# First MLP, combined pairs of weight tiles: four PSUM banks, another order of products, one tile of 1024 columns for the four results

## The chip, the cores and the metric

One core of one Trainium2 chip runs the whole program. The metric is the device time of one execution in microseconds (us); below 0.2% (about 3.4 us) two times of this kernel cannot be told apart.

## The reference

```python
# linear attention with an RMS norm, x is [4608, 512]
kv  = einsum('bhsd,bhse->bhde', k, v);  o = einsum('bhsd,bhde->bhse', q, kv)
x   = o / sqrt(mean(o*o) + 1e-6) * g_norm          # heads side by side
# first MLP, 512 -> 2048 -> 512
h   = x @ w_in
x   = (h * clip(h + 3, 0, 6) / 6) @ w_out
# second MLP, 512 -> 1536 -> 512
out = (silu(x @ w_gate) * (x @ w_val)) @ w_out2
```

## The kernel before

All matrix products that need accuracy are made of three products of a high and a low part (hi and lo) of each operand. The helper `split` makes the two: ScalarE (ACT) writes hi (L109), VectorE (DVE) writes lo as the difference (L110).

The first MLP goes through nine blocks of 512 tokens, j = 0 to 8. Block 0, and the first half of block 1, multiply weight tile by weight tile (`h_whole`, L119). From there on two weight tiles (a pair, p) and the two halves of a block are multiplied together by a scheme of seven products in place of eight (`hpair`), on sums and differences of the operands (A11, S1, ... of the weights, made by `combine`; B11, T1, ... of the block, made by `prepare_x1`). There are 60 such pairs: four in block 1, eight in each of the blocks 2 to 8.

A product (`product`, L654) is six matmuls of 256 columns into one PSUM bank. `hpair` works with three banks a, c and d out of the pool `pmm`, which has four; the fourth is free for the attention of the next block. Seven products run in the order a, c, a, d, c, a, d. ACT copies the first results out of a and c into s, v and u (L566, L568, L570), DVE adds d to v (L572), and at the end four adds on DVE (L576 to L579) form the four quarters of the result in two tiles h0 and h1 of 512 columns. Bank a is used three times: the product S2 x T2 adds onto the first one as soon as s has been copied, and A12 x B21 starts anew as soon as u has been copied.

Each of the two tiles is then gated: ACT computes t = relu(h + 3) (L582), DVE computes min(t, 6) * h (L583), and `split_g` makes hi and lo of it, the operand g of the second matrix product `o_pair` (L113 to L115, 24 matmuls of 512 columns for one pair). There is one buffer of t, and three of g.

The order of TensorE's (PE's) work is written out by hand; that of ACT and DVE comes from a planner at build time, and each engine then runs its list strictly in order. On PE, iteration i of a block issues `hpair` of pair i, then a piece of the attention of the next block (at i = 0, 1, 3 and 4 the matmuls `kv` of a head pair, L253, where the next block opens a new batch, and at i = 1, 2, 4 and 5 `at`, both into banks of `pmm`), then `o_pair` of pair i - 1. At i = 0 there is no `o_pair`, so pair 1 of a block follows pair 0 at once, or with only `kv` between them. At the last i, `o_pair` comes twice, and `prepare_x1` of the next block is issued between the two. `kv` is read out of its bank by two splits of 64 x 64, one for each head (ACT, DVE, ACT, DVE). In the last block, j = 8, each iteration also loads, decodes and combines a part of the second MLP's weights on ACT and DVE (`load_second`), and the first operands of the second MLP are prepared (`prepare_x`, L625).

The second MLP's `quad` does the same seven products with four banks of its own, 384 columns wide, and takes two of `hpair`'s tiles as scratch.

Of the kernel before, what the change touches and what calls it, by code (L numbers as in the profile page):

```python
# [8 lines left out]
F32 = mybir.dt.float32  # L9
F32R = mybir.dt.float32r  # L10
U32 = mybir.dt.uint32
AF = mybir.ActivationFunctionType
ALU = mybir.AluOpType
# [5 lines left out]
def kernel(  # L19
# [27 lines left out]
    nc = tc.nc  # L47
    P = 128
# [9 lines left out]
    TQ = T // 2  # L58
# [7 lines left out]
    TH = 384  # L66
    T2 = 2 * TH
# [29 lines left out]
    hpool = ctx.enter_context(tc.tile_pool(name="h1", bufs=1, side="right"))  # L97
# [3 lines left out]
    pmm = mlp1.enter_context(tc.tile_pool(name="pmm", bufs=4, space=PSUM))  # L101


    def f32(ap):
        return ap.bitcast(F32)

    def split(hi, lo, src):

        nc.scalar.activation(out=hi, in_=src, func=AF.Copy)  # L109
        nc.vector.tensor_tensor(out=lo, in0=src, in1=f32(hi), op=ALU.subtract)  # L110
# [16 lines left out]
    three = const.tile([P, 1], F32, name="three")  # L127
# [285 lines left out]
    def split_g(j, f, src):  # L413
        g = gpool.tile([P, 2, T], F32R, tag="g", name=f"g_{j}_{f}")
        split(g[:, 0], g[:, 1], src)
        g_t[j, f] = g
# [131 lines left out]
    def product(ps, w, x, first):  # L548
        n = 0
        for kk in range(2):  # L550
            for a, b in ((w[0], x[1]), (w[1], x[0]), (w[0], x[0])):
                nc.tensor.matmul(
                    ps, a[:, kk], b[:, kk], start=first and n == 0, stop=n == 5,
                    skip_group_check=True,
                )
                n += 1

    def hpair(j, p):

        n = f"{j}_{p}"  # L560
        h = [hpool.tile([P, 2, TQ], F32, tag=f"h{i}", name=f"h{i}_{n}") for i in range(2)]
        s, u, v = (hpool.tile([P, TQ], F32, tag=o, name=f"{o}_{n}") for o in "suv")
        a, c, d = (pmm.tile([P, 512], F32, tag="mm", name=f"{o}_{n}")[:, :TQ] for o in "acd")
        w, x = ready[p], xo1
        product(a, w["A11"], x["B11"], True)
        nc.scalar.activation(out=s, in_=a, func=AF.Copy)  # L566
        product(c, w["S1"], x["T1"], True)
        nc.scalar.activation(out=v, in_=c, func=AF.Copy)  # L568
        product(a, w["S2"], x["T2"], False)
        nc.scalar.activation(out=u, in_=a, func=AF.Copy)  # L570
        product(d, w["S3"], x["T3"], True)
        nc.vector.tensor_tensor(out=v, in0=v, in1=d, op=ALU.add)  # L572
        product(c, w["S4"], x["B22"], False)
        product(a, w["A12"], x["B21"], True)
        product(d, w["A22"], x["T4"], False)
        nc.vector.tensor_tensor(out=h[0][:, 1], in0=u, in1=c, op=ALU.add)  # L576
        nc.vector.tensor_tensor(out=h[0][:, 0], in0=s, in1=a, op=ALU.add)  # L577
        nc.vector.tensor_tensor(out=h[1][:, 1], in0=v, in1=u, op=ALU.add)
        nc.vector.tensor_tensor(out=h[1][:, 0], in0=u, in1=d, op=ALU.add)  # L579
        for i in range(2):  # L580
            t = hpool.tile([P, 2, TQ], F32, tag="t", name=f"t_{n}")
            nc.scalar.activation(out=t, in_=h[i], func=AF.Relu, bias=three[:, 0:1])  # L582
            nc.vector.scalar_tensor_tensor(  # L583
                out=t, in0=t, scalar=6.0, in1=h[i], op0=ALU.min, op1=ALU.mult
            )
            split_g(j, 2 * p + i, t.rearrange("p n c -> p (n c)"))

    def hpair_whole(j, p):
        h_whole([2 * p], j)
# [70 lines left out]
    def quad(name, w, xo):  # L660

        h = big["h"].tile([P, 4, TH], F32, tag="h", name=f"h{name}")
        u, v = (hpool.tile([P, TH], F32, tag=f"h{i}", name=f"h{i}{name}") for i in range(2))

        a, e, c, d = (
            big["ps"].tile([P, 512], F32, tag=f"q{i}", name=f"q{i}_{name}")[:, :TH] for i in range(4)
        )
        product(c, w["S1"], xo["T1"], True)
        product(d, w["S3"], xo["T3"], True)
        nc.scalar.activation(out=v, in_=c, func=AF.Copy)  # L670
        nc.vector.tensor_tensor(out=v, in0=v, in1=d, op=ALU.add)
        product(a, w["A11"], xo["B11"], True)
        nc.scalar.activation(out=u, in_=a, func=AF.Copy)
        product(e, w["S2"], xo["T2"], True)
        nc.vector.tensor_tensor(out=u, in0=u, in1=e, op=ALU.add)
        product(c, w["S4"], xo["B22"], False)
        product(d, w["A22"], xo["T4"], False)
        nc.vector.tensor_tensor(out=h[:, 3], in0=v, in1=u, op=ALU.add)
        nc.vector.tensor_tensor(out=h[:, 1], in0=u, in1=c, op=ALU.add)
        nc.vector.tensor_tensor(out=h[:, 2], in0=u, in1=d, op=ALU.add)  # L680
        product(a, w["A12"], xo["B21"], False)
        nc.scalar.activation(out=h[:, 0], in_=a, func=AF.Copy)  # L682
        return h

    def gv_step(c, j, p, xo):
        hg = quad(f"g_{c}", wgv["g", p], xo)
        nc.scalar.activation(out=hg, in_=hg, func=AF.Silu)
        hv = quad(f"v_{c}", wgv["v", p], xo)
        nc.vector.tensor_tensor(out=hv, in0=hg, in1=hv, op=ALU.mult)  # L689
        nc.sync.dma_start(  # L690
            out=g2d[2 * p:2 * p + 2, :, j * T2:(j + 1) * T2].rearrange("f p t -> p f t"),
            in_=hv.rearrange("p (f n) c -> p f (n c)", f=2),
        )
# [152 lines left out]
    with tc.manual_schedule(engines={mybir.EngineType.PE}):  # L846
# [13 lines left out]
        for h in range(2):  # L860
            nc.sync.dma_start(
                out=gn[h * D:(h + 1) * D, :], in_=g_norm.rearrange("(p o) -> p o", o=1)
# [145 lines left out]
        for j in range(1, NB):  # L1008
# [3 lines left out]
            for i, p in enumerate(pairs):  # L1012
                if j == 1 and p < PWHOLE:
                    hpair_whole(j, p)
                    make_wi(p + PWHOLE)
                    if p == PWHOLE - 1:
                        prepare_x1(j)
                else:
                    hpair(j, p)
                    if j == 2 and i < PWHOLE:  # L1020
                        make_wi(i)
# [64 lines left out]
        for c, (n, j, p) in enumerate(steps):  # L1086
            i = c % NH
# [8 lines left out]
            if n < NB2:  # L1096
                m = (n + 1) % NB2
                if i < 2:
                    tiles = load_half(*halves[m], i)
                    if i and m:  # L1100
                        for k, t in enumerate(tiles):
                            nc.sync.dma_start(
                                out=wsd[m - 1, k], in_=f32(t).rearrange("p k f -> p (k f)")
# [81 lines left out]
```

## Time and profile before

| | us |
|---|---|
| median of 3 runs | 1703.4 (1702.52 to 1703.5) |
| the profiled execution's own time | 1705.95 |
| its span, first to last instruction | 1704.2 |
| PE busy | 1668.5 (98%) |
| DVE busy | 1321.0 (78%) |
| ACT busy | 813.8 (48%) |
| granted TensorE clock, mean | 0.996 |

An engine's busy time counts its instructions, overlaps once. PEld is the loading of weights into TensorE, which runs beside the matmuls; a matmul that has to wait shows first as a wait of its weight load. The first MLP's combined pairs stand between 198 and 888 us of the span, the last block of them between 796 and 888 us.

### The profile page before, as it was taken

Reading aid. Unit: us, or ns where it says so; the run is one execution under the profiler, and the core shown is the slowest. Engines: PE = TensorE matmul, PEld = TensorE weight load, DVE = VectorE, ACT = ScalarE, POOL = GpSimd, SP = SyncE. Lnnn points to the kernel's source line nnn. Section 1 sums busy time; section 2 is a strip of 40 time slices with the busy share of each in tenths; the row PEclk is TensorE's granted clock in tenths of the full one; section 3 lists DMA queues with packets and bytes.
Section 4 is the critical chain, followed back from the end, with each engine's and each line's share of the span. In section 5 each row is a group of like instructions: output and inputs, shape, how many; then the busy total and the mean of one; then the engine's idle time right before and its main releaser. Section 6 shows DMA issues by size and latency. Waiting matters only on the chain.

```text
span 1704.2 us, 27886 instructions
## 1 busy us (share of the span) xinstructions
PE 1668.5 (98%) x10608; PEld 1522.4 (89%) x10608; DVE 1321.0 (78%) x2531; ACT 813.8 (48%) x1489; POOL 2.4 (0%) x7
## 2 busy tenths in 40 slices
PE   7999999999999999999999999999999999999999
PEld 3566789899988989998889999999999999999998
DVE  5897987777777767776889988778898677877774
ACT  4565554445445454545555544443554444443432
POOL 0000000000000000000000000000000000000000
PEclk8999999999999999999999999999999999999999
DMA  7886444454544544425454544485444457555643
GB/s 191 246 258 189 128 145 129 129 161 114 164 131 144 143 149 113 128 99 173 161 186 167 216 161 161 148 278 204 149 178 156 142 204 277 198 193 192 215 147 103
DMA packets 224951, 288.63 MB, mean 169 GB/s; under 512 B 80944, under 2 KB 139312, under 8 KB 224816
## 3 DMA queue, kind: packets, MB, share of 16 engines
q1 hardware_dynamic: 224816, 286.85, 52.4%
q8 instruction: 83, 1.36, 0.3%
q14 instruction: 52, 0.43, 0.1%
HBM read 211.03 MB, written 75.76 MB: 168 GB/s over the span
## 4 chain that ended last, share of the span: by engine, by line
PE 81%; DVE 10%; DMA 4%; ACT 3%; issue 2%; SPq 1%; DVEq 0%; ACTq 0%
PE q_g L654 15%; PE q_v L654 14%; PE acc L113 7%; PE acc L114 7%; PE acc L115 7%; PE a L654 6%; PE d L654 4%; PE c L654 4%; PE h L119 3%; PE o2d L795 3%; PE o2a L795 3%; PE o2c L795 3%; PE o2e L795 1%; DMA gb<-g2d 1%; PE kv L253 1%
## 5 line engine op out<-in xcount | busy, mean ns | idle before, releaser
L113 PE MATMUL acc<-g,wo 128*128 128x512 f32 x512 | 202.1, 395 | 0.0
L114 PE MATMUL acc<-g,wo 128*128 128x512 f32 x512 | 199.9, 390 | 0.0
L115 PE MATMUL acc<-g,wo 128*128 128x512 f32 x512 | 199.5, 390 | 0.0
L582 ACT ACTIVATE t<-h,three 128x512 f32<-128x512 f32 x120 | 86.7, 723 | 138.9 <-DVE h L577 109.4
L109 ACT ACTIVATE g<-t 128x512 fp32r<-128x512 f32 x144 | 90.9, 631 | 87.4 <-DVE t L583 73.4
L110 DVE TENSOR_TENSOR g<-t,g 128x512 fp32r<-128x512 f32 x144 | 98.0, 681 | 31.5 <-ACT g L109 31.2
L115 PEld LDWEIGHTS acc<-g,wo 128*128 128x128 f32 x512 | 96.1, 188 | 20.5
L113 PEld LDWEIGHTS acc<-g,wo 128*128 128x128 f32 x512 | 96.2, 188 | 20.0
L114 PEld LDWEIGHTS acc<-g,wo 128*128 128x128 f32 x512 | 96.2, 188 | 18.3
L583 DVE SCALAR_TENSOR_TENSOR t<-t,h 128x512 f32<-128x512 f32 x120 | 82.6, 689 | 19.3 <-ACT t L582 15.7
L119 PE MATMUL h<-x,w_i 128*128 128x512 f32 x192 | 87.0, 601 | 1.9 <-DVE w_i L173 1.9
L119 PEld LDWEIGHTS h<-x,w_i 128*128 128x128 f32 x192 | 36.7, 193 | 43.2 <-issue 40.2
L682 ACT ACTIVATE hg<-q_g 128x384 f32<-128x384 f32 x36 | 17.8, 494 | 117.1 <-PE q_g L654 117.1
L654 PE MATMUL q_v<-hT,v 128*128 128x384 f32 x288 | 73.6, 336 | 0.0
L110 DVE TENSOR_TENSOR lT<-T,hT 128x384 fp32r<-128x384 f32 (+1 forms) x120 | 68.0, 588 | 0.8 <-ACT hT L109 0.2
L654 PE MATMUL a<-lB,wh_i 128*128 128x256 f32 x240 | 68.1, 284 | 0.0
L654 PE MATMUL a<-hB,wh_i 128*128 128x256 f32 x240 | 67.9, 283 | 0.0
L654 PE MATMUL a<-hB,wl_i 128*128 128x256 f32 x240 | 67.9, 283 | 0.0
L572 DVE TENSOR_TENSOR v<-v,d 128x256 f32<-128x256 f32 x60 | 25.1, 419 | 54.3 <-PE d L654 54.1
L689 DVE TENSOR_TENSOR hv<-hg,hv 128x1536 f32<-128x1536 f32 x36 | 63.1, 1754 | 5.1 <-ACT hv L682 4.9
L109 ACT ACTIVATE hT<-T 128x384 fp32r<-128x384 f32 (+1 forms) x120 | 60.5, 548 | 2.7 <-DVE T L625 2.5
L682 ACT ACTIVATE hv<-q_v 128x384 f32<-128x384 f32 x36 | 17.8, 494 | 87.2 <-PE q_v L654 87.2
(558 smaller groups left out, 5448.0 us busy)
## 6 DMA issues: line engine op xcount, KB each, us to landing
wo<-wod SPq DMA_DIRECT2D x128, 512.0 KB, 3.5
g2d<-hv SPq DMA_DIRECT2D x36, 768.0 KB, 3.5
graw<-g2d SPq DMA_DIRECT2D x26, 1024.0 KB, 7.3
xr<-x1d SPq DMA_DIRECT2D x11, 1536.0 KB, 7.0
gb<-g2d SPq DMA_DIRECT2D x54, 256.0 KB, 5.4
x1d<-x1o SPq DMA_DIRECT2D x36, 256.0 KB, 3.6
out_dram<-o SPq DMA_DIRECT2D x36, 256.0 KB, 2.5
raw_i<-in_moe_w_in_dram SPq DMA_DIRECT2D x16, 512.0 KB, 5.6
```

Of the source, the lines that this page charges most:

```text
L109: nc.scalar.activation(out=hi, in_=src, func=AF.Copy)
L110: nc.vector.tensor_tensor(out=lo, in0=src, in1=f32(hi), op=ALU.subtract)
L113: nc.tensor.matmul(out_, wh, xl, start=start, stop=False)
L114: nc.tensor.matmul(out_, wl, xh, start=False, stop=False)
L115: nc.tensor.matmul(out_, wh, xh, start=False, stop=stop)
L119: nc.tensor.matmul(out_, f32(w), f32(x), start=start, stop=stop)
L582: nc.scalar.activation(out=t, in_=h[i], func=AF.Relu, bias=three[:, 0:1])
L583: nc.vector.scalar_tensor_tensor(out=t, in0=t, scalar=6.0, in1=h[i], op0=ALU.min, op1=ALU.mult)
L654: nc.tensor.matmul(ps, a[:, kk], b[:, kk], start=first and n == 0, stop=n == 5, skip_group_check=True,)
L682: nc.scalar.activation(out=h[:, 0], in_=a, func=AF.Copy)
L689: nc.vector.tensor_tensor(out=hv, in0=hg, in1=hv, op=ALU.mult)
L795: nc.tensor.matmul(ps[:, i * TO2:(i + 1) * TO2], a[:, cs], b, start=first and i == 0 and n == 0, stop=n == 2, skip_group_check=True,)
```

## The change

`hpair` takes all four banks of `pmm`: S2 x T2 gets a bank e of its own, and A12 x B21 adds onto A11 x B11 in bank a, so that the copy s is gone. The order of the products becomes c, d, a, e, c, d, a. ACT copies v, u and, after the last product, the first quarter; DVE adds d to v, e to u, then v + u, u + c and u + d. The four quarters lie in one tile h of 1024 columns with one buffer, and v is its last quarter. The gate is one operation of 1024 columns on ACT and one on DVE, on one tile t with one buffer. The SBUF that these tiles take is the same in sum (9 KB per partition). `quad`'s scratch tiles take other names, since h0 and h1 no longer exist.

```diff
-        h = [hpool.tile([P, 2, TQ], F32, tag=f"h{i}", name=f"h{i}_{n}") for i in range(2)]
-        s, u, v = (hpool.tile([P, TQ], F32, tag=o, name=f"{o}_{n}") for o in "suv")
-        a, c, d = (pmm.tile([P, 512], F32, tag="mm", name=f"{o}_{n}")[:, :TQ] for o in "acd")
+        h = hpool.tile([P, 4, TQ], F32, tag="h", name=f"h_{n}")
+        u, v = hpool.tile([P, TQ], F32, tag="u", name=f"u_{n}"), h[:, 3]
+        e, c, d, a = (pmm.tile([P, 512], F32, tag="mm", name=f"{o}_{n}")[:, :TQ] for o in "ecda")
         w, x = ready[p], xo1
-        product(a, w["A11"], x["B11"], True)
-        nc.scalar.activation(out=s, in_=a, func=AF.Copy)
         product(c, w["S1"], x["T1"], True)
         nc.scalar.activation(out=v, in_=c, func=AF.Copy)
-        product(a, w["S2"], x["T2"], False)
-        nc.scalar.activation(out=u, in_=a, func=AF.Copy)
         product(d, w["S3"], x["T3"], True)
         nc.vector.tensor_tensor(out=v, in0=v, in1=d, op=ALU.add)
+        product(a, w["A11"], x["B11"], True)
+        nc.scalar.activation(out=u, in_=a, func=AF.Copy)
+        product(e, w["S2"], x["T2"], True)
+        nc.vector.tensor_tensor(out=u, in0=u, in1=e, op=ALU.add)
         product(c, w["S4"], x["B22"], False)
-        product(a, w["A12"], x["B21"], True)
         product(d, w["A22"], x["T4"], False)
-        nc.vector.tensor_tensor(out=h[0][:, 1], in0=u, in1=c, op=ALU.add)
-        nc.vector.tensor_tensor(out=h[0][:, 0], in0=s, in1=a, op=ALU.add)
-        nc.vector.tensor_tensor(out=h[1][:, 1], in0=v, in1=u, op=ALU.add)
-        nc.vector.tensor_tensor(out=h[1][:, 0], in0=u, in1=d, op=ALU.add)
+        nc.vector.tensor_tensor(out=v, in0=v, in1=u, op=ALU.add)
+        nc.vector.tensor_tensor(out=h[:, 1], in0=u, in1=c, op=ALU.add)
+        product(a, w["A12"], x["B21"], False)
+        nc.vector.tensor_tensor(out=h[:, 2], in0=u, in1=d, op=ALU.add)
+        nc.scalar.activation(out=h[:, 0], in_=a, func=AF.Copy)
+        t = hpool.tile([P, 4, TQ], F32, tag="t", name=f"t_{n}")
+        nc.scalar.activation(out=t, in_=h, func=AF.Relu, bias=three[:, 0:1])
+        nc.vector.scalar_tensor_tensor(
+            out=t, in0=t, scalar=6.0, in1=h, op0=ALU.min, op1=ALU.mult
+        )
         for i in range(2):
-            t = hpool.tile([P, 2, TQ], F32, tag="t", name=f"t_{n}")
-            nc.scalar.activation(out=t, in_=h[i], func=AF.Relu, bias=three[:, 0:1])
-            nc.vector.scalar_tensor_tensor(
-                out=t, in0=t, scalar=6.0, in1=h[i], op0=ALU.min, op1=ALU.mult
-            )
-            split_g(j, 2 * p + i, t.rearrange("p n c -> p (n c)"))
+            split_g(j, 2 * p + i, t[:, 2 * i:2 * i + 2].rearrange("p n c -> p (n c)"))
...
-        u, v = (hpool.tile([P, TH], F32, tag=f"h{i}", name=f"h{i}{name}") for i in range(2))
+        u, v = (hpool.tile([P, TH], F32, tag=o, name=f"{o}{name}") for o in ("h", "t"))
```

## Rows read from the trace of the kernel before

**Rows 1.** The page, engines: busy us, share of the span, instructions.
```profile
PE 1668.5 (98%) x10608; PEld 1522.4 (89%) x10608; DVE 1321.0 (78%) x2531; ACT 813.8 (48%) x1489; POOL 2.4 (0%) x7
```

**Rows 2.** Table by stage: length, busy us of each engine (instructions), granted clock, DMA.
```profile
230.00:796.00 566.00, 563.36 (x3807) 508.41 (x3806) 417.81 (x941) 273.27 (x548) 0.00 (x0) 1.00 0.47 136
796.00:888.00 92.00, 85.85 (x531) 76.92 (x530) 75.64 (x158) 50.52 (x96) 0.00 (x0) 1.00 0.51 173
888.00:1704.00 816.00, 806.15 (x5294) 799.96 (x5292) 643.04 (x1044) 364.35 (x609) 0.00 (x0) 1.00 0.53 185
```

**Rows 3.** Waits of weight loads, 190 to 232 us: total us, times, longest.
```profile
PEld a L654 <- ACT s L566: 1.3, 3, 0.6
```

**Rows 4.** Waits of weight loads, 232 to 796 us.
```profile
PEld a L654 <- ACT s L566: 2.5, 5, 0.5
PEld d L654 <- DVE v L572: 2.0, 4, 0.6
```

**Rows 5.** Waits of weight loads, 796 to 890 us (block 8).
```profile
PEld d L654 <- DVE v L572: 4.4, 3, 1.7
PEld a L654 <- ACT s L566: 2.9, 3, 1.7
```

**Rows 6.** PE timeline, block 6 begins at 617.69: start us, us, instruction.
```profile
606.78 0.40 PE L113 MATMUL acc<-g,wo 128*128 128x512 f32 x1
...
617.69 0.28 PE L654 MATMUL a<-lB,wh_i 128*128 128x256 f32 x1
...
619.12 0.30 PE L654 MATMUL a<-lT,wh_i 128*128 128x256 f32 x1
619.26 0.28 PE L654 MATMUL a<-hT,wl_i 128*128 128x256 f32 x1
...
622.82 0.57 PE L253 MATMUL kv<-vA,kA 128*64 128x64 f32 x12
...
623.55 0.39 PE L654 MATMUL a<-lB,wh_i 128*128 128x256 f32 x1
```

**Rows 7.** ACT timeline of the same stretch.
```profile
618.60 0.38 ACT L566 ACTIVATE s<-a 128x256 f32<-128x256 f32 x1 [0.79 <-PE a L654]
...
622.73 0.72 ACT L582 ACTIVATE t<-h,three 128x512 f32<-128x512 f32 x1 [2.29 <-DVE h L577]
623.67 0.22 ACT L109 ACTIVATE kvbd<-kv 64x64 fp32r<-64x64 f32 x1 [0.22 <-PE kv L253]
624.21 0.63 ACT L109 ACTIVATE g<-t 128x512 fp32r<-128x512 f32 x1 [0.32 <-DVE t L583]
624.86 0.22 ACT L109 ACTIVATE kvbd<-kv 64x64 fp32r<-64x64 f32 x1
```

**Rows 8.** DVE timeline of the same stretch.
```profile
624.87 0.69 DVE L110 TENSOR_TENSOR g<-t,g 128x512 fp32r<-128x512 f32 x1 [0.57 <-ACT g L109]
625.60 0.23 DVE L110 TENSOR_TENSOR kvbd<-kv,kvbd 64x64 fp32r<-64x64 f32 x1
```

**Rows 9.** Instructions by line and form: busy us, mean ns, idle before.
```profile
L109 ACT ACTIVATE g<-t 128x512 fp32r<-128x512 f32 x144 | 90.9, 631 | 87.4 <-DVE t L583 73.4 <-DVE t L427 11.9 <-PE acc L115 1.0
L582 ACT ACTIVATE t<-h,three 128x512 f32<-128x512 f32 x120 | 86.7, 723 | 138.9 <-DVE h L577 109.4 <-DVE g L110 29.3
L583 DVE SCALAR_TENSOR_TENSOR t<-t,h 128x512 f32<-128x512 f32 x120 | 82.6, 689 | 19.3 <-ACT t L582 15.7
L110 DVE TENSOR_TENSOR gxl<-gt,gxh 128x1024 fp32r<-128x1024 f32 x26 | 31.8, 1224 | 7.8 <-ACT gxh L109 7.8
L109 ACT ACTIVATE gxh<-gt 128x1024 fp32r<-128x1024 f32 x26 | 27.4, 1054 | 47.5 <-DVE gt L723 47.5
```

**Rows 10.** DVE timeline of block 8.
```profile
801.06 0.56 DVE L625 TENSOR_TENSOR T<-xr 128x384 f32<-128x384 f32 x1 [3.81 <-DMA x1d<-x1o]
801.54 0.41 DVE L572 TENSOR_TENSOR v<-v,d 128x256 f32<-128x256 f32 x1
...
819.68 0.42 DVE L572 TENSOR_TENSOR v<-v,d 128x256 f32<-128x256 f32 x1
```

## Prediction

> **What bounds the kernel now.** The page's first part: PE is busy 98% of the span, DVE 78%, ACT 48% [rows 1]. The table by stage says where the other 2% could be had. Between 230 and 796 us, in the pairs of the blocks 1 to 7, PE stands idle 566.00 - 563.36 = 2.6 us, while DVE has 148 us free and ACT 293; in block 8 (796 to 888) PE is idle 6.2 us of 92, with DVE busy 82%; behind it, in the second MLP, PE is idle 10 us of 816 [rows 2]. The clock is full in all three. So what the change does to the load of ACT and DVE is worth nothing by itself: it has to remove waits of PE, and what it removes there reaches the end, since PE is filled after it.
>
> Next the waits, read at the weight loads, because a late product shows there in full. In the pairs they name two instructions: the second product into bank a waits for the copy s, and A22 x T4 into bank d waits for v + d. From 190 to 232 us s takes 1.3 us (3 times) [rows 3]; from 232 to 796 us s 2.5 us (5 times) and v + d 2.0 us (4 times) [rows 4]; in block 8 v + d 4.4 us (3 times) and s 2.9 us (3 times) [rows 5]. Together 13.1 us: this is all that the pairs could give, 0.8% of the time.
>
> Last the timelines around the start of a block, the **seam**, where pair 1 follows pair 0 without an `o_pair` between them. A product takes (619.12 - 617.69) / 2 = 0.72 us, seven take 5.04, so pair 0 ends at 622.73; `kv` follows and pair 1 starts at 623.55 [rows 6]. Elsewhere an `o_pair` of (617.69 - 606.78) / 2 = 5.45 us stands between two pairs [rows 6]. ACT works at the seam through the gate of pair 0 and the splits of `kv`, and so comes late to the copy s of pair 1. I put the five waits of 0.5 us for s [rows 4] there: one for each of the blocks 2 to 6, the ones whose seam has a `kv`.
>
> **The change part by part.**
>
> *Instructions.* PE keeps its 42 matmuls in each pair. Three copies on ACT stay three, five adds of 256 columns on DVE stay five. The two gate operations on ACT are 2 x 723 = 1446 ns; the one of 1024 columns I estimate as 723 plus what a copy grows by from 512 to 1024 columns, 1054 - 631 = 423: 1146 ns [rows 9]. On DVE 2 x 689 = 1378 become 1224 ns, the row of another two-operand instruction of 1024 columns [rows 9]. Saved are 0.30 and 0.15 us a pair, 18 and 9 us over 60 pairs, on engines that are not the bound: 0. No DMA is added or moved, on no queue. The scratch of `quad` has other names and the same single buffers: 0.
>
> *Bank e and the order, inside a pair.* S2 x T2 no longer waits for any copy. v, u and v + d now have three products (2.16 us) between what they read and the product that needs the bank again; before it was one for s and two for the others. Removed: the waits for s from 190 to 232 us, 1.3; the waits for v + d up to 796 us, 2.0, none of which is longer than 0.6, under the 0.72 of the added product. A third sum: the first matmul of S2 x T2 is followed 0.14 us later by the next, where the spacing is 0.12 [rows 6], the copy s landing just in time; 0.02 to 0.03 us in some 50 pairs, 1.3 us. Together 4.6 us, with 3 and 5 as its ends.
>
> *Block 8, outside its seam.* There v + d is late because DVE has a queue of decoding in front of it (at 819.68 us in pair 2 [rows 10]), not because of its own operand. The order of the products asks for d at the sixth place instead of the seventh, 0.72 us earlier, and one more product follows it. If DVE's list stays as it is, each of these waits grows by 0.72 and the product behind it is moved out: a loss of about 0.35 us a pair. If the planner, which now has v + d ready 1.44 us earlier, puts it before the backlog, the wait goes. One wait of each kind belongs to the block's seam, where v + d runs late at 801.54 us [rows 10]; I give these two about a third of the sums, 1.4 and 0.8, which leaves 5.1 us of waits for the rest of the block [rows 5]; I take 40%, 2.0 us, with -1 and 5.1 as the ends.
>
> *What is late next: the seam.* Here the change adds two waits.
>
> First, v is now a quarter of h, which has one buffer: the copy v of pair 1 may not start before DVE's gate of pair 0 has read h. The chain, on the clock of [rows 6]: the last product ends at 622.73; the copy of the first quarter starts 0.2 us later (as s does: 617.69 + 0.72 = 618.41 to 618.60 [rows 7]) and takes 0.38, to 623.31; the gate's ACT half, after 0.1, to 624.56; DVE's half, after 0.05, to 625.83; v from 625.9 to 626.3. The fifth product of pair 1 needs it at 623.55 + 4 x 0.72 = 626.43. That just holds if nothing stands before v on ACT; but the two splits of g, 0.63 each [rows 7], become ready at the same 625.83, and whatever of them goes first delays v, and behind it u, the first quarter's copy and with them PE: 0 to 1.1 us. In the blocks 7 and 8 there is no `kv`, pair 1 starts 0.8 us earlier, and the wait is 0.7 to 1.9 us.
>
> Second, the banks. Before, pair and `kv` together used the four banks. Now pair 0 uses all, `kv` takes one of them, and pair 1 asks for all four within its first four products, the last of which starts at 625.71. `kv`'s bank is freed in turns of ACT, DVE, ACT, DVE; it came free at 625.60 + 0.23 = 625.83 [rows 8], with DVE's gate of 689 ns in front of it. With 1224 ns in front the first DVE turn falls behind 625.83 and ends at 626.05; the second turns add 0.5 if they go at once, and 1.8 behind a split of g on each engine (0.63 and 0.69 [rows 7, 8]): 626.55 to 627.9. Fourth asker: 0.85 to 2.2 us late; third asker: 0.7 more, up to 2.9. This wait covers the first one. I take 1.4 us, in the lower half because the planner did put `kv`'s splits between those of g [rows 7].
>
> Away from the seam `o_pair`'s 5.45 us cover both chains. At the end of a block `o_pair` of the last pair asks for g 5.45 us after the pair's end; the longer gate (0.2 + 0.38 + 0.1 + 1.15 + 1.22, then 0.63 and 0.69 for hi and lo) gives it at 4.5: free, with 1 us to spare.
>
> *The sum.* Blocks 1 to 7: -4.6. Block 8 outside the seam: -2.0. Five seams with `kv`: 1.4 in place of 0.5, +4.5. Seam of block 7: +1.1, the middle of 0.7 to 1.9 less something. Seam of block 8: +0.5, since 2.2 us of waits stand there already, where DVE stood 3.81 us for a DMA [rows 10]. Sum: -0.5 us. The profiled span of 1704.2 becomes 1703.7 and its own time 1705.95 about 1705.4; that execution was 2.5 us above the median of 1703.4, which becomes **1702.9**. With a seam wait of s us the change is about 6.6 - 1.6 + 2.5 - 5s = 7.5 - 5s us faster.
>
> **A rule against the trace.** The waits of the pairs come back in the same place, at the second use of bank a, 8 times up to 796 us [rows 3, 4]. The Trainium skill, page "Perfetto Trace Analysis", section "Optimizing Tensor Performance", says that independent groups of matmuls should rotate through different PSUM banks so that the evacuation of one overlaps the next group's matmuls. By that, bank e takes away every wait for s and the change gains up to the 13.1 us. It speaks as well against the change: with all four banks in one pair there is nothing left to rotate into for `kv` and the next pair.
>
> **The rivals.**
>
> *The seam is cheap* (faster). The planner puts `kv`'s splits ahead of DVE's gate, or v ahead of g's splits, and s is about 0.4: 5.5 us faster, 1698. For it: ACT and DVE both had idle time of 0.2 to 0.6 us just there [rows 7, 8]. Against it: what the program writes first, the gate, went first before.
>
> *Every wait goes*, as by the rule above: 13.1 + 1.3 us, 1689. For it: each wait names an operation that gets more room. Against it: block 8's queue on DVE [rows 2, 10].
>
> *The seam decides* (slower). `kv`'s bank is the third asked for, and both splits of g go before its last turns: s = 2.9, 7.5 - 14.5 = 7 us slower, 1710. For it: one buffer of h, and a pool with no free bank. It decides from s = 2.2 on (3.4 us slower).
>
> *Block 8 keeps its waits*: -1 in place of 2.0, the sum 3 us worse, 1706, not to be told from no change.
>
> **How the numbers follow.** A measurement of this kernel can tell 0.2%, 3.4 us, from no change. Within it (my forecast with block 8 either way, own range 1700 to 1706.8): 0.38. The cheap seam 0.27 and every wait gone 0.05: faster 0.32. The dear seam: 0.30. The range for 8 in 10 runs from the cheap seam with most of block 8's waits gone (1696) to the dear one (1710).
>
> **What would show it.** After the change no weight load waits for s, and those for v + d up to 796 us are gone. At the seams of the blocks 2 to 6 PE waits in pair 1: for the split of `kv` or for v, and how long is s. In block 8 the count and length of waits for v + d tell whether DVE's list changed. The stage from 888 us to the end stays at 816 us; if it grows, a gain was given back there. Wrong would be the sum, not the size of its terms, if the planner's new lists on ACT and DVE made waits in pairs that have an `o_pair` before them.

## Result: slower, by 0.8%

The changed kernel takes 1717.5 us (1715.33 to 1720.33) against 1703.45 us (1702.52 to 1705.48) of the kernel before in the same runs: a ratio of the fast runs of 1.0076, interval 1.0060 to 1.0092 (the two medians alone give 1.0083). Forecast were 1702.9 us, with 1696 to 1710 as the range. The changed kernel's profiled execution took 1717.95 us, its span 1716.2, which is 12.0 us more than before on both counts. The medians lie 14.1 us apart, mostly because the profiled execution of before was 2.5 us above its median. The account below is of the 12.0.

The page's engines after, and the table by stage (length, busy us of each engine, granted clock, DMA), to be held against [rows 1, 2]:

```profile
PE 1674.3 (98%) x10608; PEld 1528.6 (89%) x10608; DVE 1315.9 (77%) x2471; ACT 793.0 (46%) x1429; POOL 2.4 (0%) x7
...
230.00:796.00 566.00, 553.85 (x3748) 500.70 (x3747) 406.15 (x879) 251.13 (x489) 0.00 (x0) 0.99 0.45 132
796.00:888.00 92.00, 86.85 (x520) 77.89 (x519) 70.08 (x137) 44.24 (x83) 0.00 (x0) 0.96 0.50 169
888.00:1716.00 828.00, 820.16 (x5363) 812.48 (x5362) 655.49 (x1067) 372.83 (x624) 0.00 (x0) 1.00 0.53 185
```

ACT and DVE have less to do, as forecast: 813.8 to 793.0 and 1321.0 to 1315.9 us, and the wide gate takes 1151 ns on ACT and 1211 on DVE where 1146 and 1224 were estimated. It buys nothing. Between 230 and 796 us PE is now idle 12.2 us, where it was 2.6, and the granted clock is no longer 1.00 in the first two stages. The 828 us of the last row are no loss of the second MLP: the row begins at a fixed time, and some 13 us of late first MLP have moved into it. In the second MLP the clock falls once, at 1454 us; in a control without the change (the 57 buffers of experiment 10) it falls at 1442 us, so this fall is not put down to the change.

The longest waits of the weight loads between 190 and 900 us, after (total us, times, longest), to be held against [rows 3 to 5]:

```profile
PEld e L654 <- DVE kvbd L110: 11.5, 5, 2.3
PEld c L654 <- ACT h L566: 4.4, 2, 2.7
PEld acc L113 <- issue: 2.5, 1, 2.5
PEld d L654 <- DVE h L568: 1.9, 5, 0.6
```

Every wait for s is gone and those for v + d fall from 6.4 to 1.9 us: the change does what it says. Three new waits stand in their place. Bank e waits for `kv`'s split, once in each of the blocks 2 to 6. Bank c waits for the copy v (which now writes h, L566), at the seams of the blocks 7 and 8. And one `o_pair` waits 2.15 us for something that the weight-load view calls "issue"; PE's own view of the waits names it, a DMA:

```profile
PE acc L113 <- DMA wo<-wod: 2.1, 1, 2.1
```

**The seam.** ACT, DVE and PE after, at the seam of block 6, which the changed kernel reaches some 8 us later than [rows 6 to 8]:

```profile
631.25 0.38 ACT L579 ACTIVATE h<-a 128x256 f32<-128x256 f32 x1 [2.49 <-PE a L654]
631.66 1.15 ACT L581 ACTIVATE t<-h,three 128x1024 f32<-128x1024 f32 x1
632.72 0.20 ACT L109 ACTIVATE kvbd<-kv 64x64 fp32r<-64x64 f32 x1
634.11 1.15 ACT L109 ACTIVATE g<-t 128x512 fp32r<-128x512 f32 x2 [1.19 <-DVE t L582]
635.28 0.22 ACT L109 ACTIVATE kvbd<-kv 64x64 fp32r<-64x64 f32 x1
635.52 0.38 ACT L566 ACTIVATE h<-c 128x256 f32<-128x256 f32 x1
...
632.85 1.23 DVE L582 SCALAR_TENSOR_TENSOR t<-t,h 128x1024 f32<-128x1024 f32 x1 [1.89 <-ACT t L581]
633.99 0.21 DVE L110 TENSOR_TENSOR kvbd<-kv,kvbd 64x64 fp32r<-64x64 f32 x1
634.77 1.29 DVE L110 TENSOR_TENSOR g<-t,g 128x512 fp32r<-128x512 f32 x2 [0.57 <-ACT g L109]
636.09 0.23 DVE L110 TENSOR_TENSOR kvbd<-kv,kvbd 64x64 fp32r<-64x64 f32 x1
...
636.38 0.39 PE L654 MATMUL e<-lT,wh_i 128*128 128x256 f32 x1 [2.09 <-DVE kvbd L110]
```

DVE's gate of the whole tile ends at 634.08, and both halves of g (x2 in one row) go ahead of `kv`'s second turn, on ACT and on DVE. `kv`'s bank is free at 636.09 + 0.23 = 636.32, and the first matmul into e starts at 636.38. Before, one half of g stood there [rows 7, 8]; the gate of the other half started on DVE only when `kv`'s last split had ended:

```profile
626.41 0.69 DVE L583 SCALAR_TENSOR_TENSOR t<-t,h 128x512 f32<-128x512 f32 x1 [0.58 <-ACT t L582]
```

The wait has the same size, 2.24 to 2.25 us, in all five blocks.

**The clock.** Ten us at the seams of the blocks 3, 4, 5 and 6 (same columns as the table by stage):

```profile
350.00:360.00 10.00, 7.91 (x65) 7.51 (x64) 6.01 (x12) 4.11 (x10) 0.00 (x0) 0.83 0.21 59
445.00:455.00 10.00, 7.91 (x69) 7.13 (x68) 7.62 (x16) 5.68 (x13) 0.00 (x0) 1.00 0.26 76
540.00:550.00 10.00, 8.65 (x61) 8.06 (x62) 6.66 (x14) 5.06 (x12) 0.00 (x0) 0.83 0.11 28
633.00:643.00 10.00, 7.91 (x70) 7.22 (x70) 7.55 (x14) 5.44 (x12) 0.00 (x0) 1.00 0.27 78
```

After the wait of 2.24 us the granted clock falls in the blocks 3 and 5 and stays full in 4 and 6. PE's timeline of block 3 has the fall, within the product into c that follows the one into e:

```profile
353.70 0.38 PE L654 MATMUL e<-lT,wh_i 128*128 128x256 f32 x1 [2.09 <-DVE kvbd L110]
...
354.88 0.28 PE L654 MATMUL c<-lB,wh_i 128*128 128x256 f32 x1
355.00 0.32 PE L654 MATMUL c<-hB,wl_i 128*128 128x256 f32 x1
355.12 0.41 PE L654 MATMUL c<-hB,wh_i 128*128 128x256 f32 x1
...
356.61 0.41 PE L654 MATMUL a<-lB,wh_i 128*128 128x256 f32 x1
356.82 0.41 PE L654 MATMUL a<-hB,wl_i 128*128 128x256 f32 x1
```

From 355.12 on the matmuls follow each other in 0.21 us instead of 0.12 and show 0.41 instead of 0.28: the lower of the clock's two levels, 1.2 in place of 2.4 GHz. In the kernel before the same two blocks have full clock. The Trainium skill, page "TensorE: Matmul & The Clock Gate", section "HAM oscillation — how this bites in real kernels", says that a wait of PE can bring the clock down, so that the work after it starts cold. In its example this happens behind every wait; here it happens behind the waits of the blocks 3 and 5 and not behind the equal ones of 4 and 6.

**The list of SP.** SP (SyncE) issues the transfers, in the order of a list of its own. What it issues around the end of block 7, before and after (start, us, line), and PE there, after:

```profile
788.40 0.32 SPq L447 DMA_DIRECT2D wo<-wod  x1
788.82 0.58 SPq L599 DMA_DIRECT2D xr<-x1d  x1
791.12 0.33 SPq L447 DMA_DIRECT2D wo<-wod  x1
```

```profile
799.42 0.59 SPq L599 DMA_DIRECT2D xr<-x1d  x1
800.25 5.76 SPq L447 DMA_DIRECT2D wo<-wod  x3
...
805.27 0.39 PE L115 MATMUL acc<-g,wo 128*128 128x512 f32 x1
807.80 0.47 PE L113 MATMUL acc<-g,wo 128*128 128x512 f32 x1 [2.15 <-DMA wo<-wod]
...
809.84 0.63 PE L114 MATMUL acc<-g,wo 128*128 128x512 f32 x1
```

Each block loads 16 tiles `wo` of 512 KB, the weights of its second product. Before, the last of block 7 goes out at 788.40, and the 1.5 MB load of xr, the second MLP's first input, behind it; the one at 791.12 is block 8's. After, xr stands ahead of block 7's last `wo`, the first of the three at 800.25, which is wanted at once. PE's matmuls on it start 7.55 us after its issue, where the page's median landing for `wo` is 3.6 us. Behind that wait, too, the clock is halved (0.63 instead of 0.39).

**The account.** PE is filled from pair to pair, so a delay shows as a shift of the starts of the pairs. Starts of the first matmul of some pairs, from the two timelines of PE:

```
block, pair     before     after     after - before
1, 4            197.96    198.32      +0.36
2, 1 / 2, 2     255.54 / 268.40   255.68 / 270.33   +0.14 / +1.93
3, 1 / 3, 2     347.59 / 360.40   349.20 / 365.30   +1.61 / +4.90
4, 1 / 4, 2     439.06 / 451.95   443.60 / 458.27   +4.54 / +6.32
5, 1 / 5, 2     531.22 / 544.16   536.84 / 553.08   +5.62 / +8.92
6, 1 / 6, 2     623.55 / 636.50   631.87 / 646.62   +8.32 / +10.12
7, 1 / 7, 2     714.58 / 725.84   724.65 / 737.74  +10.07 / +11.90
7, 7 / 8, 0     780.42 / 796.36   792.28 / 811.97  +11.86 / +15.61
8, 1 / 8, 2     802.82 / 814.13   817.24 / 831.98  +14.42 / +17.85
8, 7            872.12    885.56     +13.44
end of span    1704.2    1716.2      +12.0
```

The five seams cost 1.79, 3.29, 1.78, 3.30 and 1.80 us, 12.0 in sum; 1.5 us more where the clock fell. The seam of block 7 costs 1.83, the end of block 7 (DMA and clock) 3.75, the seam of block 8 (from pair 0 to pair 2) 2.24. The rest of block 8 gains 4.4 (pair 2 to pair 7), the rest of the pairs of the blocks 1 to 7 2.3, of which 0.36 only make up for a later first pair, and what follows gains 1.4.

### The profile page after: what moved, and what is told of

Same layout as the page of the kernel before. It is cut to its first block, busy times and chain, and to the rows that moved or that the text cites. A ratio compares the mean times of both kernels' runs of the same rounds, so it can differ in the third digit from the quotient of the medians.

```text
span 1716.2 us, 27812 instructions
## 1 busy us (share of the span) xinstructions
PE 1674.3 (98%) x10608; PEld 1528.6 (89%) x10608; DVE 1315.9 (77%) x2471; ACT 793.0 (46%) x1429; POOL 2.4 (0%) x7
## 4 chain that ended last, share of the span: by engine, by line
PE 81%; DVE 9%; DMA 4%; ACT 3%; issue 2%; SPq 0%; DVEq 0%; ACTq 0%
PE q_g L654 14%; PE q_v L654 14%; PE acc L113 7%; PE acc L114 7%; PE acc L115 7%; PE d L654 4%; PE a L654 4%; PE c L654 4%; PE h L119 4%; PE o2d L795 3%; PE o2a L795 3%; PE o2c L795 3%; PE e L654 2%; PE o2e L795 1%; DMA gb<-g2d 1%
## 5 line engine op out<-in xcount | busy, mean ns | idle before, releaser
L109 ACT ACTIVATE g<-t 128x512 fp32r<-128x512 f32 x144 | 86.7, 628 | 66.4 <-DVE t L582 47.3
L582 DVE SCALAR_TENSOR_TENSOR t<-t,h 128x1024 f32<-128x1024 f32 x60 | 72.7, 1211 | 31.4 <-ACT t L581 30.9
L579 ACT ACTIVATE h<-a 128x256 f32<-128x256 f32 x60 | 23.0, 383 | 126.7 <-PE a L654 126.2
L581 ACT ACTIVATE t<-h,three 128x1024 f32<-128x1024 f32 x60 | 69.1, 1151 | 10.4 <-DVE h L578 8.1
```

The lines of the kernel that those rows point to most:

```text
L581: nc.scalar.activation(out=t, in_=h, func=AF.Relu, bias=three[:, 0:1])
L582: nc.vector.scalar_tensor_tensor(out=t, in0=t, scalar=6.0, in1=h, op0=ALU.min, op1=ALU.mult)
```

## Experiments

Theory at this point: five waits for `kv`'s bank, a second wait for v close behind each, the halved clock and SP's list make up the loss, and the new inside of the pair is a gain. Rival: the wide gate, or the new lists as such, are the loss. Where a tile was added, one of the 58 buffers of the pool `w` was given up for it (kernels 2, 3, 4 and 8); the others have 58. Kernels are compared with each other by their medians; kernels 1 to 4, then 6, 8 and 9, then 5, 7 and 11 ran together, each group with its own runs of the kernel before (medians 1704.3, 1703.0 and 1704.4 us).

**1. `kv`'s bank alone.** At the seam `kv` takes a bank of the second product's accumulators, which is free there:

```diff
-        ps = pmm.tile([P, 512], F32, tag="mm", name=f"kv_{b}_{hp}")
+        if b > 2 and hp == 0:
+            ps = pacc.tile([P, 512], F32, tag="acc0", name=f"kv_{b}_{hp}")
+        else:
+            ps = pmm.tile([P, 512], F32, tag="mm", name=f"kv_{b}_{hp}")
```

> The kv of a block's first iteration goes into an idle accumulator bank instead of one of pmm's four. Theory (the seam's wait is for kv's bank, freed late behind the gate of 1024 columns): the five waits of 2.25 us of bank e for the split of kv vanish; the copy v then decides in these seams, about 1.1 us each, as v waits for the gate to have read h; no stretch at half clock in blocks 3 and 5 (1.5 us each): about 5 x 1.15 + 3 = 9 us faster than the changed kernel, 1708 us. Rival (PE waits for ACT and DVE's gate whatever the bank): a wait as long for another releaser in the same place, 1716 to 1719 us.

Measured: 1708.4 us, 1.0023 of before (1.0013 to 1.0033), 9 us under the changed kernel. Its waits of weight loads:

```profile
PEld c L657 <- ACT h L569: 10.3, 7, 2.8
PEld acc L113 <- issue: 2.6, 1, 2.6
```

No wait for `kv`, and behind it appears the wait for v, seven times instead of twice: 1.11 us at each of the five seams by PE's timeline (5.8 of the 10.3 us of weight-load waits are theirs). The clock is 1.00 from 230 to 796 us.

**2. v alone.** v gets a tile of its own, and only v + u writes the last quarter of h:

```diff
-        u, v = hpool.tile([P, TQ], F32, tag="u", name=f"u_{n}"), h[:, 3]
+        u, v = (hpool.tile([P, TQ], F32, tag=o, name=f"{o}_{n}") for o in "uv")
...
-        nc.vector.tensor_tensor(out=v, in0=v, in1=u, op=ALU.add)
+        nc.vector.tensor_tensor(out=h[:, 3], in0=v, in1=u, op=ALU.add)
```

> v gets a tile of its own (the room comes from one of 58 weight buffers). Theory (v, as a quarter of h with one buffer, waits for the gate of the pair before): the waits of bank c for the copy v in pair 1 of the blocks 7 and 8 (1.65 and 2.64 us) vanish, with the stretch at half clock after the second (1.5 us); the five waits of 2.25 us for kv's bank stay: about 1712 us. Rival (the copy is late because of what stands before it on ACT, not because of h): both waits stay, 1717 us.

Measured: 1715.4 us, 1.0058 (1.0042 to 1.0074). The waits for v are gone and those for `kv` stay, 2.3 us each, with the clock down again behind the seams of the blocks 3 and 5 (0.83 in the same ten us). Expected were 1712 us: the waits for v went as the theory said, but the wait for `wo` is longer here, 3.4 us, and the 2 us between this time and the changed kernel's are not clear of the noise.

**3. Both.** The two diffs above together.

> Both edits together. Theory: no wait over 0.5 us is left in any pair 1; 11.3 + 4.3 us of waits and three to four stretches at half clock (about 5 us) go: 1697 us, faster than the kernel before by about 6. The wait of 2.3 us for a DMA of wo at the end of block 7 stays, it has another cause. Rival (four banks and the order gain nothing inside the pairs): 1703 us or more.

Measured: **1695.3 us** (1694.55 to 1696.35), 0.9944 (0.9927 to 0.9961), faster than both kernels. Its waits of weight loads from 190 to 900 us, and its stages:

```profile
PEld acc L113 <- issue: 2.7, 2, 2.5
PEld d L657 <- DVE v L571: 2.2, 5, 1.0
```

```profile
230.00:796.00 566.00, 563.66 (x3817) 509.30 (x3816) 412.92 (x895) 256.62 (x498) 0.00 (x0) 1.00 0.46 138
796.00:888.00 92.00, 91.24 (x566) 82.94 (x565) 81.94 (x164) 51.39 (x95) 0.00 (x0) 1.00 0.56 183
```

One edit gains 9 us, the other 2, both together 22: the two waits stand one behind the other at each seam, and the longer one hides the other. The starts of the pairs show it without the noise of the medians: from pair 1 of block 2 to pair 1 of block 7 the changed kernel falls 9.9 us behind before, kernel 1 2.0, kernel 2 10.4, and kernel 3 gets 4.5 us ahead. Against before the five seams now gain 0.55 us each by the starts of the pairs: the old wait for s [rows 4]. The wide gate is still there, so it need not be a loss once both waits are gone.

**4. SP's list, on top of both.** The load of xr is issued behind the last `wo`:

```diff
+                if j == NB - 1 and i == 0:
+                    wo_prev = wo_last[0]
...
-                        x1 = load_x1(0)
+                        with tc.issue_after(wo_prev.ins):
+                            x1 = load_x1(0)
```

> Both edits, and the load of x1 for the second MLP (1.5 MB) is queued on SP behind the last load of wo of block 7, as it stood in the kernel before. Theory (the 2.3 us wait for wo comes from the 1.5 MB ahead of it): that wait goes, with 1.5 us at half clock behind it: 3 to 4 us less than with both edits alone, about 1693.5 us. Rival (the wait comes from the buffer of wo, which is freed late): the wait stays, within 1 us of both edits alone.

Measured: 1696.0 us, 0.9948 (0.9933 to 0.9963): no gain. The wait for `wo` is gone, and in its place the waits for v + d rise from 2.2 to 5.3 us:

```profile
PEld d L661 <- DVE v L575: 5.3, 8, 1.5
```

By the starts of the pairs it is 3.3 us ahead of kernel 3 at the start of block 8 (-4.37 against -1.05 us, relative to before) and level with it at pair 7 (-7.43 against -7.50). In block 8 DVE is the next limit, and what PE does not wait for at its start it waits for later. Behind the first MLP kernel 4's profile loses 2.2 us on kernel 3's; the clock falls there once (0.83 from 1430 to 1440 us, 1.00 in kernel 3), as in a control without the change (experiment 10).

**5. SP's list, in the changed kernel.** The diff of 4 alone.

> The changed kernel with the 1.5 MB load of x1 queued on SP behind block 7's last load of wo, and nothing else. Theory (the change's new list on SP costs a wait of 2.3 us for wo and 1.5 us at half clock): both go, 3.8 us less, 1713.5 us. With both seam edits the same edit gave 0.7 us the other way, as the waits for v + d in block 8 grew to 5.3 us; rival: the same happens here, 1717 us, with more than 4 us of waits for v + d in block 8.

Measured: 1715.4 us, 1.0062 (1.0038 to 1.0086), not to be told from the changed kernel (1.0076, 1.0060 to 1.0092; in the same group, kernel 11, 1.0083, 1.0058 to 1.0109). The wait for `wo` is gone; the longest wait for v, at the seam of block 8, grows from 2.7 to 3.4 us:

```profile
PEld c L658 <- ACT h L570: 5.1, 2, 3.4
```

The rival's waits for v + d did not come: they are 1.0 us in block 8, not over 4. By the starts of the pairs this profile is 3.3 us ahead of the changed kernel's at the start of block 8 and still 2.7 at its pair 7, with the clock down at three seams instead of two. So in the profile most of the wait stays gained, but the times cannot tell the theory's 3.8 us from nothing.

**6. The gate in two.** The changed kernel with v's own tile and the gate as it was, two operations of 512 columns on each engine:

```diff
-        t = hpool.tile([P, 4, TQ], F32, tag="t", name=f"t_{n}")
-        nc.scalar.activation(out=t, in_=h, func=AF.Relu, bias=three[:, 0:1])
...
+        for i in range(2):
+            hi = h[:, 2 * i:2 * i + 2]
+            t = hpool.tile([P, 2, TQ], F32, tag="t", name=f"t_{n}_{i}")
+            nc.scalar.activation(out=t, in_=hi, func=AF.Relu, bias=three[:, 0:1])
...
```

> The changed kernel with v in a tile of its own and the gate undone to two operations of 512 columns with a buffer of 512 (kv stays in pmm's four banks). Theory (it is the long gate in front of kv's first DVE turn, and the two splits of g that it releases at once, that free kv's bank late): kv's bank comes free 8.1 us after pair 0's start, as in the kernel before, bank e asks for it at 8.0: the five waits fall from 2.3 us to 0.2 to 0.6 us and no half clock follows them; with the wait for wo still there about 1700 us. Rival (any kernel that gives all four banks to a pair waits 2 us for kv's): 1713 to 1716 us.

Measured: 1707.4 us, 1.0020 (1.0010 to 1.0030): 8 us under kernel 2 (6.5 by the ratios to before), from which it differs by the gate and by one buffer in the pool `w`, which is worth nothing by itself (experiment 10). Its waits:

```profile
PEld d L655 <- DVE v L568: 5.0, 6, 2.8
PEld e L655 <- DVE kvbd L110: 4.7, 5, 0.9
```

The wait for `kv` falls from 2.3 to 0.9 us, since now one half of g goes ahead of `kv`'s second turn instead of two; none of the five is followed by a lower clock. So 1.4 of the 2.3 us are the wide gate's, and 0.9 are there with the narrow one. The time lies between the theory's 1700 us and the rival's 1713 to 1716: the waits stayed longer than the 0.2 to 0.6 us expected, and by the starts of the pairs the end of block 7, with the wait for `wo` and a lower clock behind it, costs 4.2 us.

**7. The gate in two, with both edits.** The diffs of 1, 2 and 6 together.

> Both seam edits (v of its own, kv of a block's first iteration in an accumulator bank) with the gate undone to operations of 512 columns; 58 weight buffers. Theory (ACT and DVE are not the bound, the width gives nothing once the seams are free): within 2 us of both edits with the wide gate, 1693 to 1698 us. Rival (the shorter gate is what made both edits faster than the kernel before): 1700 us or more.

Measured: 1703.0 us, 0.9988 (0.9977 to 0.9998), 7.7 us over kernel 3, where little difference was expected: the time that the rival gave, 1700 us or more. The seams are as free as in kernel 3, and from pair 1 of block 2 to pair 7 of block 7 the two gain nearly the same on before, 4.9 and 4.6 us. The difference comes behind that: at the end of block 7, which by the starts of the pairs costs 4.2 us against before instead of 2.3, the wait for `wo` being followed by a lower clock here and not in kernel 3, and in block 8, in one wait of 2.83 us for v + d. PE and DVE there:

```profile
830.41 0.38 PE L658 MATMUL d<-lT,n_i 128*128 128x256 f32 x1 [2.83 <-DVE v L571]
...
829.34 0.69 DVE L110 TENSOR_TENSOR wl_v<-w_v,wh_v 128x512 fp32r<-128x512 f32 x1
829.94 0.41 DVE L571 TENSOR_TENSOR v<-v,d 128x256 f32<-128x256 f32 x1
```

v + d stands behind a piece of weight decoding in DVE's list, as in pair 2 of before [rows 10]. Whether that is the gate's width, or only how these lists came out, one kernel doesn't tell; so of kernel 3's 9 us under before it is open how much the banks and the order would give with the narrow gate; and the two spans differ by 4.8 us, so about 3 us of the medians' difference are in neither profile.

**8. The wide gate alone, in the kernel before.** Old order, three banks, h and t as one tile each:

```diff
-        h = [hpool.tile([P, 2, TQ], F32, tag=f"h{i}", name=f"h{i}_{n}") for i in range(2)]
+        h = hpool.tile([P, 4, TQ], F32, tag="h", name=f"h_{n}")
...
+        t = hpool.tile([P, 4, TQ], F32, tag="t", name=f"t_{n}")
+        nc.scalar.activation(out=t, in_=h, func=AF.Relu, bias=three[:, 0:1])
```

> The kernel before with three banks and its own order of products, and only the gate changed: one h and one t of 1024 columns (s, u and v keep their own tiles; 57 weight buffers instead of 58 make the room). Theory (width alone costs little, since kv then has a bank of its own; but s of pair 1 may come behind the wider operations on ACT): five seams at 0.5 to 1.2 us, the list on SP puts the load of x1 before wo as in the changed kernel: 1703 to 1708 us. Rival (the wide gate is what makes the change slow, with or without the bank): 1712 us or more.

Measured: 1709.8 us, 1.0035 (1.0021 to 1.0049), 1706.1 us of span against 1704.2. The profiled execution is the fastest of its five, the medians lie 6.8 us apart. The five waits for s at the seams of the blocks 2 to 6 are gone. New are a wait of 2.4 us for `wo` and a wait of 0.8 us for s at the seam of block 7; at the seam of block 8 the wait for s is 1.7 us where it was 0.8:

```profile
PEld a L654 <- ACT s L566: 4.8, 7, 1.7
PEld acc L113 <- issue: 2.7, 1, 2.7
```

By the starts of the pairs the end of block 7 costs 4.3 us and block 8 gives 3.1 back. The time lies between the theory (1708 us at most) and the rival (1712 or more): the wide gate alone makes the kernel before slower, by half of the change's loss, and the largest loss in its profile comes with SP's list and the clock behind the wait for `wo`.

**9. u in a quarter of h.** As kernel 3, with v in its own tile and u in the first quarter of h, which needs no SBUF more; `kv` as in 1.

```diff
-        u, v = hpool.tile([P, TQ], F32, tag="u", name=f"u_{n}"), h[:, 3]
+        v, u = hpool.tile([P, TQ], F32, tag="u", name=f"v_{n}"), h[:, 0]
```

> As with both edits, but the room for v comes from u, which moves into the first quarter of h (58 weight buffers). u is needed 1.44 us later than v was, so of the waits for the gate in pair 1 nothing or at most 0.3 us stays in blocks 2 to 6, and up to 0.9 in 7 and 8. Theory: 1695 to 1698 us. Rival (the gain of both edits came from the changed number of weight buffers): 1704 us or more.

Measured: 1698.4 us, 0.9974 (0.9964 to 0.9985). The seams stay free; one `o_pair` waits 1.1 us for g at 245 us, and the waits for v + d are 3.4 us instead of 2.2. With all 58 buffers in the pool `w` it is still faster than before, so the gain of kernel 3 is not that of the buffer given up.

**10. Controls.** The kernel before with 57 buffers in the pool `w`:

> The kernel before with 57 instead of 58 weight buffers, to see what that part of the edits does by itself: every theory has 1703.5 us, within 1.5.

Measured: 1704.1 us, 1.0004 (0.9994 to 1.0013). The kernel before with the edit of kernel 1, `kv` in an accumulator's bank:

> The kernel before, with nothing of the change, and only the seam's kv moved from the pool of four banks into the bank acc0 of the second product's accumulators: a control for the run that had kv's bank and v's own tile and took 1695.3 us. Theory (that gain is the change's own, set free by the two edits): in the kernel before no wait names kv, the five waits at the seams are for the copy s behind ACT's splits, 0.5 us each, and stay; 1703.5 us, within 2 us. Rival (the gain is that of kv's bank alone, whatever the order of the products): the seam waits go and the time falls below 1700, to 1696 at the lowest.

Measured: 1703.8 us, 0.9994 (0.9985 to 1.0004). So neither what kernel 3 gave up nor what it borrowed is the gain: in the kernel before each of the two is worth nothing.

**11. The changed kernel again.**

> The changed kernel once more beside the others, for a second profile: five waits of bank e of 2.2 to 2.3 us, and stretches at half clock behind some of the waits over 2 us, not behind those under 1.7 us; 1717 us.

Measured: 1718.8 us, 1.0083 (1.0058 to 1.0109). All five seams wait 2.24 to 2.25 us as in the first profile, but the clock now falls behind four of them (blocks 2, 3, 5 and 6). Two of the ten us at a seam, blocks 3 and 4:

```profile
350.00:360.00 10.00, 7.92 (x66) 7.51 (x65) 5.40 (x11) 3.67 (x8) 0.00 (x0) 0.83 0.23 64
445.00:455.00 10.00, 7.91 (x90) 7.47 (x90) 5.96 (x12) 5.24 (x11) 0.00 (x0) 1.00 0.20 59
```

## Why the prediction was wrong

**What held, in part.** The inside of the pair. The waits for s and nearly all for v + d up to 796 us went, and the last wait for v + d in each of the blocks 2 to 5 came back as 0.3 to 0.7 us of earlier starts. In block 8 the planner did move v + d: in pair 2 it now runs at 833.68 us, as soon as PE has finished d (DVE stood idle for 0.37 us before it), and 4.4 us were gained outside the seam, where 2.0 were taken with 5.1 as the end. The gates' durations held within 13 ns, and no pair with an `o_pair` before it got a new wait of over 0.6 us; but the last `o_pair` of block 1 now waits 0.6 us for g, where the prediction had "1 us to spare". So the blocks 1 to 7 gave 2.3 us for 4.6. The third sum of 1.3 us, the copy "landing just in time", was not there: over the pairs 2 to 6 of the blocks 3 to 6 the starts shift by 0.04 us or less.

**The term that was mis-sized: the wait for `kv`'s bank.** The prediction had the mechanism, the place, and the bounds "Fourth asker: 0.85 to 2.2 us late", and took 1.4 since the planner "did put `kv`'s splits between those of g". It did so with a gate in two parts, where the second half of g was not ready yet. With one gate both halves are ready at the same moment, and both went first: 2.25 us, just over the upper end. The narrow gate waits 0.9 us (kernel 6); that this is near the lower end is chance, since the 0.85 was worked out for the wide gate with `kv`'s turns ahead of both halves of g. By the prediction's own formula 2.25 gives 7.5 - 5 x 2.25 = -3.8, slower, 1707 us: the side of the rival "the seam decides", by its order of the splits though not by its third asker. Those 1707 us still lie in the range of 1696 to 1710. What carried the time past it are the two things below that had no term in the sum, the clock (3.0 us at these seams alone) and SP's list (3.75). The Trainium skill's page "Perfetto Trace Analysis" says under "Optimization Strategy" that the same gap, repeating, can mean too little PSUM for the next tile; five gaps of 2.25 us that end with the release of a bank, and that go with one bank more (kernel 1), are that case.

**A second wait under the first.** "This wait covers the first one" was right, and kernel 1 shows its size, 1.11 us, the upper end of "0 to 1.1". In the blocks 7 and 8, where nothing covers it, it was 1.65 and 2.64 us. Block 7 cost 1.83 for the 1.1 taken, within its bounds; block 8's seam cost 2.24 for 0.5.

**What was missing: the clock.** "The clock is full in all three" was read from the kernel before and carried over as if it were a property of the stage. It went down behind some of the new waits, four times up to the end of block 8. By the starts of the pairs that is 1.5 us each time: 3.0 at the seams of the blocks 3 and 5, and part of the 3.75 at the end of block 7 and of block 8's seam.

**What was missing: SP's list.** "No DMA is added or moved, on no queue" is true of the program's text. But SP's list is planned like the others and came out in another order: 3.75 us at the end of block 7. What turned the order stays open: the wait is there with the wide gate alone (kernel 8) and with the narrow gate and four banks (kernel 6), and in neither control. Nor is it sure to be had by itself: in kernel 4 the waits in block 8 took it back; in kernel 5 2.7 us of it were left at the end of block 8 by the profile, and the times do not tell.

In sum, against the forecast terms: seams of blocks 2 to 6 12.0 for 4.5, block 7's seam 1.8 for 1.1, block 8's seam 2.2 for 0.5, the list 3.75 for 0, blocks 1 to 7 inside, with the later first pair, -1.9 for -4.6, block 8 -4.4 for -2.0, all behind -1.4 for 0: 12.0 for -0.5.

**Shown and argued.** Shown by a run: the waits for the bank and for v, and that removing both takes 22 us off, with the clock that goes with them (kernels 1 to 3); the share of the gate's width in the bank's wait (kernel 6); that the wait for `wo` comes from the load ahead of it (kernels 4 and 5). Read from profiles and not from an edit: that the clock alone costs 1.5 us a time. It rests on comparing seams of one profile, and on the seam of block 6, which costs 1.8 us in the first profile of the changed kernel and 3.3 in the second, with the same wait. Open: why the narrow gate is 7.7 us dearer than the wide one once the seams are free, when the wide one alone costs the kernel before 6.8; and what the four banks and the new order give each by itself, since no run has one without the other.

## What to carry to other kernels

When a change takes the last free buffer of a shared pool, name everyone else who draws on the pool, and price the neighbour's wait at the upper end unless the order of the releasing engine is known for the new program. Where two waits end close together, plan to remove both: one edit alone moved 2 (within the noise) or 9 us here, both 22. And in a kernel whose lists come from a planner, a row of the old trace that rests on the order of a list (a split between two others, a load behind another) is not a fact about the new kernel.

## What the hardware did that was not expected

Equal waits were followed by unequal clocks. In the four profiles whose five seams wait 2.2 to 2.3 us, the clock fell behind 2, 2, 3 and 4 of the five (the changed kernel, kernel 2, kernel 5, the changed kernel again), not at the same blocks; each time the start of the next pair shifts by some 3.3 us instead of 1.8. Behind the five waits of 0.9 us in kernel 6 it never fell. So a wait of PE can cost two thirds more than its length, and one execution of a program differs from another by that: the two profiles of the changed kernel, with two and four falls at these seams, have spans of 1716.2 and 1719.3 us.
